# Fused linear attention and gated MLP on one core: fills, splits, load issues and transposes moved between engines and queues

## Chip, cores and metric

One core of one Trainium2 chip. The metric is the device time of one launch in microseconds (us). Kernels are timed in alternation with the kernel before on the same chip. The executions of one kernel over 1.5% above the fastest of the same kernel are classed as slow and left out of the ratios.

## The reference, cut to what matters

For 8 batches, 8 heads, 576 tokens and head width 64, the first stage is linear attention with features exp(p) and exp(-p), where p is a projection shifted by its largest absolute value. The second is an MLP whose gate mixes tokens.

```python
def phi(x):                                   # x: (8, 8, 576, 64), w_phi: (64, 128)
    proj = np.einsum('bhsd,df->bhsf', x, w_phi)
    proj = proj - np.max(np.abs(proj), axis=-1, keepdims=True)
    return np.concatenate([np.exp(proj), np.exp(-proj)], axis=-1)
q_p, k_p = phi(q), phi(k)
kv = np.einsum('bhsf,bhsd->bhfd', k_p, v)     # and num / den with z = sum of k_p
...
h = np.maximum(x @ w_in, 0.0)                 # x: attention output, (8, 576, 512)
u, v = h[..., :512], h[..., 512:]             # v: layer norm, then a 576 x 576 token mix plus bias
gated = u * v_s
return gated @ w_out
```

## The kernel before

The work is cut into 36 units: 32 pairs of heads over the first 512 tokens of a batch, and 4 tail units that hold the last 64 tokens of two batches. Unit i is worked on in step i (keys and queries) and in the next three or four (features, sums, attention, transpose of the attention output). Tasks of the second stage wait in a list and fill TensorE between the parts of a step. After the last step the rest of the list is drained.

Four places matter. The loads of a tail or a batch, with their transposes by DMA behind them in the sync engine's queue (SP):

```python
def load_heads(b, h0, n):
    for x, t in (("k", k), ("q", q)):
        pin(nc.gpsimd.dma_start)(out=src, in_=main_ap(t, b, h0, n))       # casts to bf16
        if b >= XB:                                                       # XB = 2
            pin(nc.sync.dma_start_transpose)(out=d[x + "T"][...], in_=src...)
# load_tail(g): the same for tails: k, q by GpSimd, transposes and v by sync
# load(b): alloc, load_heads(b, 0, H), v by GpSimd for b < 2, else by sync
```

The fills of constants and, before the first unit's work is through, ten copies of bias rows, all on VectorE or left to the compiler:

```python
nc.vector.memset(vst_i, 0.0)                     # twice, 128 x 2112 bf16
nc.any.memset(vnt_i, 0.0); nc.any.memset(vnt_i[TL:TL + 1, 0, :], 1.0); ...
nc.vector.tensor_copy(out=w_spT[row, NB + bl, ...], in_=bsp_row[...])   # ten of these
```

The split of the query maxima into two bf16 parts, and the transpose of the attention output:

```python
def a_split(u):
    eng = nc.vector if u["i"] < EARLY else nc.gpsimd             # EARLY = 4
    eng.tensor_copy(out=m[:, 0:H], in_=u["mq"])                  # mq is fp32 in SBUF
    eng.tensor_tensor(out=m[:, H:2 * H], in0=u["mq"], in1=m[:, 0:H], op=ALU.subtract)

def a_x_t(u):
    if XX <= u["i"] < NU - 4:                                    # XX = 9
        nc.sync.dma_start_transpose(out=dst..., in_=u["x"]...)
        return
    # else four TensorE transposes into PSUM and one VectorE copy
```

## Time and profile before

| | |
|---|---|
| time, median of three | 302.22 us (300.67 to 305.91) |
| profiled span | 300.1 us |
| busiest engines | TensorE 87%, ScalarE 75%, VectorE 71% |
| step 0 starts (first key maximum) | 10.7 us |
| step 7 starts | 48.1 us |
| last step, 35, starts | 236.7 us |

The starts of the steps I take from VectorE's timeline: every unit begins with two reductions that give the maxima of its keys. The page and the views of this profile that carry the argument are shown in the prediction.

### The profile page before, as it was taken

The numbers are of one execution on the slowest core, as the hardware profiler recorded it, in microseconds if no ns is written. First come the engines' busy times: TensorE is split into PE (matmuls) and PEld (weight loads), VectorE is DVE, ScalarE is ACT, GpSimd is POOL, SyncE is SP. The second block draws the span as 40 slices with busy tenths as digits, with TensorE's granted clock in tenths as the row PEclk, the third lists the DMA queues.
The fourth block names the chain that finished last, engine by engine and source line by source line (L and its number), as shares of the span: only waits on it lengthen the run. The fifth ranks groups of instructions, "written<-read, shape, count | busy, mean of one in ns | idle before, by whom it ended". The sixth has DMA issues, their size and how long they took to land.

```text
span 300.1 us, 7883 instructions
## 1 busy us (share of the span) xinstructions
PE 262.3 (87%) x3007; PEld 180.4 (60%) x3046; DVE 211.9 (71%) x512; ACT 224.1 (75%) x512; POOL 184.1 (61%) x324
## 2 busy tenths in 40 slices
PE   2356888999999999779999995979999999999983
PEld 1235777576766766556667673656767667545441
DVE  5999889797968877549697883656788864445610
ACT  4336899878699997769999675879999837566033
POOL 9398388589635998447879962814988430048300
PEclk9999999999999999999999997999999999999998
DMA  9999999909952899999612999999303202600026
GB/s 142 245 153 268 166 111 159 262 1 123 215 190 75 109 166 233 152 280 162 136 21 28 185 211 224 142 305 235 81 1 37 20 2 69 226 26 0 0 84 233
DMA packets 82906, 41.10 MB, mean 137 GB/s; under 512 B 53490, under 2 KB 77234, under 8 KB 82868
## 3 DMA queue, kind: packets, MB, share of 16 engines
q1 hardware_dynamic: 55524, 27.08, 41.9%
q0 software_dynamic: 27344, 13.51, 33.1%
q8 instruction: 24, 0.39, 0.6%
q14 instruction: 14, 0.11, 0.1%
HBM read 32.85 MB, written 9.44 MB: 141 GB/s over the span
## 4 chain that ended last, share of the span: by engine, by line
PE 56%; DVE 16%; ACT 14%; DMA 8%; issue 3%; SPq 1%; ACTq 0%; DVEq 0%
PE ps L476 9%; PE pv L402 7%; PE pu L455 6%; PE po L499 6%; PE ps L236 6%; DMA out_dram<-ob 5%; ACT kf L251 5%; PE pn L353 3%; DVE mk L248 3%; DVE mq L257 3%; PE pv L333 3%; ACT qf L320 3%; PE pq L303 3%; PE pq L307 3%; PE ps L477 2%
## 5 line engine op out<-in xcount | busy, mean ns | idle before, releaser
L251 ACT ACTIVATE kf<-ps 128x512 bf16<-128x512 f32 x144 | 76.8, 667 | 19.4 <-DVE mk L248 19.1
L320 ACT ACTIVATE qf<-pq 128x512 bf16<-128x512 f32 x128 | 68.0, 667 | 13.6 <-PE pq L307 13.6
L268 POOL TENSOR_TENSOR vs<-v_f,em 128x512 bf16<-128x512 f32 x64 | 65.6, 1047 | 15.7 <-ACT em L263 15.5
L248 DVE TENSOR_REDUCE mk<-ps 128x4 f32<-128x512 f32 x72 | 46.1, 678 | 9.5 <-PE ps L236 9.2
L257 DVE TENSOR_REDUCE mq<-ps 128x4 f32<-128x512 f32 x72 | 46.3, 679 | 3.1 <-PE ps L236 2.7
L501 ACT COPY ob<-po 128x512 f32<-128x512 f32 (+1 forms) x37 | 21.6, 597 | 25.7 <-PE po L499 17.2
L405 DVE BATCH_NORM_STATS2 stats<-vr 128x6 f32<-128x512 bf16 (+1 forms) x37 | 25.2, 685 | 17.6 <-ACT vr L404 17.5
L402 PE MATMUL pv<-w_in_bf,xT 128*128 128x512 bf16 x119 | 31.2, 379 | 2.2 <-DMA xT<-x 1.7
L476 PE MATMUL ps<-w_spT,vn 128*128 128x512 bf16 x117 | 32.3, 379 | 0.6
L455 PE MATMUL pu<-xT,w_in_bf 128*128 128x512 bf16 x120 | 30.8, 379 | 0.7 <-DVE mq L257 0.3
L307 PE MATMUL pq<-mT,sel 128*128 128x128 bf16 x256 | 30.7, 222 | 0.0
L499 PE MATMUL po<-w_out_bf,uT 128*128 128x512 bf16 x121 | 29.7, 379 | 0.4 <-issue 0.2
L479 DVE TENSOR_TENSOR uT<-ps,uT 128x512 bf16<-128x512 f32 x32 | 22.1, 691 | 11.0 <-PE ps L477 9.7
L307 PEld LDWEIGHTS <-sel 128*128 128x128 bf16 x256 | 25.4, 99 | 6.5 <-issue 2.2
L344 DVE TENSOR_TENSOR x<-pn,rc 128x256 bf16<-128x256 f32 x64 | 25.8, 419 | 1.0
L287 POOL CAST mhl<-mq 128x8 bf16<-128x8 f32 x32 | 6.2, 192 | 33.1 <-DVE mq L257 29.3
L404 ACT ACTIVATE vr<-pv 128x512 bf16<-128x512 f32 (+1 forms) x37 | 23.2, 680 | 4.2 <-PE pv L402 3.3
L333 PE MATMUL pv<-vs,kf 128*128 128x66 bf16 x512 | 25.0, 195 | 0.0
L419 POOL TENSOR_SCALAR vn<-vr,rs 128x512 bf16<-128x512 bf16 x32 | 24.3, 772 | 0.8
L333 PEld LDWEIGHTS <-kf 128*128 128x128 bf16 x512 | 23.9, 99 | 1.0
L353 PE MATMUL pn<-kv,qf 128*128 128x66 bf16 x512 | 22.2, 193 | 2.0 <-ACT kf L251 0.9
L353 PEld LDWEIGHTS <-qf 128*128 128x128 bf16 x512 | 19.4, 97 | 6.0 <-issue 2.5
(127 smaller groups left out, 547.5 us busy)
## 6 DMA issues: line engine op xcount, KB each, us to landing
out_dram<-ob SPq DMA_DIRECT2D x32, 256.0 KB, 2.7
v_f<-in_v_dram SPq DMA_DIRECT2D x6, 1024.0 KB, 6.8
k_bf<-in_k_dram POOLq DMA_DIRECT2D x7, 512.0 KB, 6.7
q_bf<-in_q_dram POOLq DMA_DIRECT2D x7, 512.0 KB, 8.3
v_f<-in_v_dram POOLq DMA_DIRECT2D x2, 1024.0 KB, 8.5
v_tl<-in_v_dram SPq DMA_DIRECT2D x8, 128.0 KB, 4.2
w_in_bf<-in_moe_w_in_dram POOLq DMA_DIRECT2D x1, 1024.0 KB, 12.5
out_dram<-ob SPq DMA_DIRECT2D x8, 128.0 KB, 2.9
```

The source lines that it names most:

```text
L248: nc.vector.tensor_reduce(out=u["mk"][:, hs], in_=pk, axis=AX.X, op=ALU.max, apply_absolute_value=True)
L251: nc.scalar.activation(out=u["kf"][:, s, hs, :], in_=pk, func=AF.Exp, bias=0.0, scale=sc)
L257: nc.vector.tensor_reduce(out=u["mq"][:, 4 * half:4 * half + 4], in_=pq, axis=AX.X, op=ALU.max, apply_absolute_value=True)
L268: nc.gpsimd.tensor_tensor(out=vs[:, s, :, 0:D], in0=st[u["b"]]["v"][:, pj * H:(pj + 1) * H, :], in1=em[:, s, :].unsqueeze(2).to_broadcast( ...
L307: nc.tensor.matmul(out=pq[:, 2 * par + x, :], lhsT=sel[:, j, :], rhs=m, start=False, stop=(x == 1))
L320: nc.scalar.activation(out=qf[:, s], in_=pq, func=AF.Exp, bias=0.0, scale=sc)
L333: nc.tensor.matmul(out=pv[:, hh, s, :], lhsT=u["kf"][:, s, 4 * hh + c, :], rhs=u["vs"][:, s, 4 * hh + c, :], start=(c == 0), stop=False)
L353: nc.tensor.matmul(out=pn[:, pos, :], lhsT=u["qf"][hh][:, s, pos, :], rhs=d["kv"][:, 2 * u["pj"] + hh, s, :], start=(s == 0), stop=(s == 1))
L402: nc.tensor.matmul(out=pv[r], lhsT=lhs(kc), rhs=w_in_bf[:, kc, HALF:DFF], start=(kc == 0), stop=(kc == KC - 1))
L455: nc.tensor.matmul(out=pu, lhsT=w_in_bf[:, kc, dc * P:(dc + 1) * P], rhs=d["xT"][:, kc, :], start=(kc == 0), stop=(kc == KC - 1))
L476: nc.tensor.matmul(out=ps, lhsT=d["vn"][:, sp, cs], rhs=w_spT[:, sp, 0:T0], start=(sp == 0), stop=False)
L499: nc.tensor.matmul(out=po[r], lhsT=lhs(dc), rhs=w_out_bf[:, dc, :], start=(dc == 0), stop=(dc == KC - 1))
```

## The change

Its intent: to shorten the start, which VectorE bounds, and to take waiting transposes out of the sync queue, where stores stand behind them. The diff, cut to its core (left out: the projection's weights load from ScalarE's queue, the constants are filled in a fixed order, and half of the first tail's multiplies move to step 4):

```diff
-    TS, TB = 1, 1                      # load_tail, load: issued whole, transposes behind them
+    def load(x, b, h0=0, n=H): ...     # one operand at a time
+    def cross(b):                      # transposes of a whole batch, released on their own
+        for x in ("k", "q"): pin(nc.sync.dma_start_transpose)(out=d[x + "T"], in_=d[x]...)
...
+        pin(nc.scalar.copy)(out=vst_i, in_=zero.to_broadcast([P, 4 * H * DA]))
+        pin(nc.scalar.copy)(out=vnt_i[:, bl, :], in_=ident[:, row:row + 1].to_broadcast([P, HALF]))
...
+    load_v(0, nc.sync)                 # was: GpSimd's queue, behind tails and heads 2 and 3
+    for x in ("k", "q", "v"):
+        load_tail(x, 0)
+    load("k", 0, 2, 2); load("q", 0, 2, 2); load("k", 0, 4, 4); load("q", 0, 4, 4)
...
-    EARLY = 4; XX = 9
+    EARLY = 5; XX = 99; EK = 7         # EK: early key copies by VectorE
-            for pos, c in enumerate(POS): nc.vector.tensor_copy(... bias row ...)
+            pin(nc.scalar.copy)(... bias row, two instructions for each of two rows ...)
...
+            if early and half == 0:
+                mq = pq[:, 0, 0:H]     # the early maxima stay in PSUM and are split from there
...
-    RATE = 3.23; CAP = 1.76
+    RATE = 3.12; CAP = 2.11            # and another order of the parts of a step
...
+    AT, AB, XP = 4, 5, 2
+    at(1, load, "k", 1); at(1, load, "q", 1); at(1, load_v, 1, nc.sync)
+    at(2, load_weight, w_in_bf[:, :, HALF:DFF], ...) ; at(3, ...wsp...) ; at(4, ...)
+    # tails: k four steps ahead, q and v three; batches: k five ahead, q and v four,
+    # cross(b) two ahead; tails have no DMA transpose any more, TensorE does them
```

More of the change, by code (lines that the diff above doesn't have):

```diff
@@ L60, in pin @@
     def pin(start):
-        return lambda **kw: tc.keep_in_program_order(start(**kw))
+        return lambda *a, **kw: tc.keep_in_program_order(start(*a, **kw))
     def main_ap(t, b, h0=0, n=H):
@@ L72 @@
     gs = {}
-    TS, TB = 1, 1
     XB = 2
-    def load_tail(g):
-        d = dict(
-            q=ld.tile([P, H, D], BF16, tag="q_tl", name="q_tl", bufs=1),
-            k=ld.tile([P, H, D], BF16, tag="k_tl", name="k_tl", bufs=1),
-            v=ld.tile([P, H, D], FP32, tag="v_tl", name="v_tl", bufs=1),
-        )
-        gs[g] = d
-        for x, t in (("k", k), ("q", q)):
-            for i in range(2):
-                pin(nc.gpsimd.dma_start)(out=d[x][i * TL:(i + 1) * TL], in_=tail_ap(t, 2 * g + i))
-            if 2 * g >= XB:
-                d[x + "T"] = ld.tile([P, NP, P], BF16, tag=x + "T_t", name=x + "T_t", bufs=1)
-                pin(nc.sync.dma_start_transpose)(out=d[x + "T"], in_=d[x].rearrange("p h d -> p (h d)"))
-        for i in range(2):
-            pin(nc.sync.dma_start)(out=d["v"][i * TL:(i + 1) * TL], in_=tail_ap(v, 2 * g + i))
     def alloc(b):
@@ L98, in alloc, with alloc_tail @@
         )
-        if b >= XB:
-            for x in ("kT", "qT"):
-                st[b][x] = ld.tile([P, 2 * H, P], BF16, tag=x + "_b", name=x + "_b", bufs=2)
-    def load_heads(b, h0, n):
-        d = st[b]
-        for x, t in (("k", k), ("q", q)):
-            src = d[x][:, h0:h0 + n]
-            pin(nc.gpsimd.dma_start)(out=src, in_=main_ap(t, b, h0, n))
-            if b >= XB:
-                pin(nc.sync.dma_start_transpose)(out=d[x + "T"][:, 2 * h0:2 * (h0 + n), :],
-                                            in_=src.rearrange("p h x -> p (h x)"))
+    def alloc_tail(g):
+        gs[g] = dict(
+            q=ld.tile([P, H, D], BF16, tag="q_tl", name="q_tl", bufs=1),
+            k=ld.tile([P, H, D], BF16, tag="k_tl", name="k_tl", bufs=1),
+            v=ld.tile([P, H, D], FP32, tag="v_tl", name="v_tl", bufs=1),
+        )
@@ L112, in load_v, with load, load_tail @@
+    def load(x, b, h0=0, n=H):
+        if b not in st:
+            alloc(b)
+        pin(nc.gpsimd.dma_start)(out=st[b][x][:, h0:h0 + n], in_=main_ap(q if x == "q" else k, b, h0, n))
     def load_v(b, eng):
         pin(eng.dma_start)(out=st[b]["v"].rearrange("p (h c) d -> p h (c d)", h=H), in_=main_ap(v, b))
-    def load(b):
-        alloc(b)
-        load_heads(b, 0, H)
-        load_v(b, nc.gpsimd if b < 2 else nc.sync)
+    def load_tail(x, g):
+        if g not in gs:
+            alloc_tail(g)
+        t, eng = dict(q=(q, nc.gpsimd), k=(k, nc.gpsimd), v=(v, nc.sync))[x]
+        for i in range(2):
+            pin(eng.dma_start)(out=gs[g][x][i * TL:(i + 1) * TL], in_=tail_ap(t, 2 * g + i))
@@ new lines, in cross @@
+    def cross(b):
+        d = st[b]
+        for x in ("k", "q"):
+            d[x + "T"] = ld.tile([P, 2 * H, P], BF16, tag=x + "T_b", name=x + "T_b", bufs=2)
+            pin(nc.sync.dma_start_transpose)(out=d[x + "T"], in_=d[x].rearrange("p h x -> p (h x)"))
+    wphi_f = cpool.tile([P, F], FP32)
+    for i in range(2):
+        nc.scalar.dma_start(out=wphi_f[i * D:(i + 1) * D, :], in_=w_phi)
+    alloc(0)
+    first = {}
+    for x, t in (("k", k), ("q", q)):
+        first[x] = s2.tile([P, 2, NB * D], FP32, tag="ob", name="first", bufs=4)
+        pin(nc.sync.dma_start)(out=first[x], in_=main_ap(t, 0, 0, 2))
@@ L121 @@
     ident = cpool.tile([P, P], BF16)
     make_identity(nc, ident)
-    alloc(0)
-    for x, t in (("k", k), ("q", q)):
-        first = s2.tile([P, 2, NB * D], FP32, tag="ob", name="first", bufs=4)
-        nc.sync.dma_start(out=first, in_=main_ap(t, 0, 0, 2))
-        nc.vector.tensor_copy(out=st[0][x][:, 0:2], in_=first)
-    wphi2 = cpool.tile([P, 2 * F], BF16)
-    nc.vector.memset(wphi2, 0.0)
-    wphi_f = cpool.tile([P, F], FP32)
-    for i in range(2):
-        r = slice(i * D, (i + 1) * D)
-        nc.sync.dma_start(out=wphi_f[r, :], in_=w_phi)
-        nc.vector.tensor_copy(out=wphi2[r, i * F:(i + 1) * F], in_=wphi_f[r, :])
@@ L135 @@
-    load_tail(0)
-    load_heads(0, 2, 2)
-    load_v(0, nc.gpsimd)
-    load_heads(0, 4, 4)
+    zero = cpool.tile([P, 1], BF16)
+    pin(nc.vector.memset)(zero, 0.0)
+    wphi2 = cpool.tile([P, 2 * F], BF16)
+    pin(nc.vector.memset)(wphi2, 0.0)
+    neghalf = cpool.tile([P, NB + 1], FP32)
+    pin(nc.vector.memset)(neghalf, -0.5)
+    w_spT = cpool.tile([P, NB + 2, S], BF16)
+    pin(nc.vector.memset)(w_spT[:, NB:NB + 2, :], 0.0)
+    NM = 3
+    mhl, mT = [], []
+    for i in range(NM):
+        for tiles, name in ((mhl, "mhl"), (mT, "mT")):
+            t = cpool.tile([P, P], BF16, name=f"{name}{i}")
+            pin(nc.vector.memset)(t, 0.0)
+            tiles.append(t)
@@ new lines @@
+    sel1 = cpool.tile([P, H], BF16)
+    sel = cpool.tile([P, H, F], BF16)
+    pin(nc.vector.tensor_tensor)(out=sel1, in0=ident[:, 0:H], in1=ident[:, H:2 * H], op=ALU.add)
+    pin(nc.vector.tensor_scalar)(out=sel, in0=sel1.unsqueeze(2).to_broadcast([P, H, F]), scalar1=-1.0,
+                                 scalar2=None, op0=ALU.mult)
+    for x in ("k", "q"):
+        pin(nc.vector.tensor_copy)(out=st[0][x][:, 0:2], in_=first[x])
+    vst, vnt = [], []
+    for i in range(2):
+        t = cpool.tile([P, 2, 2, H, DA], BF16, name=f"vst{i}")
+        pin(nc.scalar.copy)(out=t.rearrange("p b s h d -> p (b s h d)"), in_=zero.to_broadcast([P, 4 * H * DA]))
+        vst.append(t)
+        if i == 0:
+            for y in range(2):
+                r = slice(y * D, (y + 1) * D)
+                pin(nc.scalar.copy)(out=wphi2[r, y * F:(y + 1) * F], in_=wphi_f[r, :])
+        t = cpool.tile([P, 2, HALF], BF16, name=f"vnt{i}")
+        for bl, row in ((0, TL), (1, 0)):
+            pin(nc.scalar.copy)(out=t[:, bl, :], in_=ident[:, row:row + 1].to_broadcast([P, HALF]))
+        vnt.append(t)
@@ L140 @@
+    load_v(0, nc.sync)
+    for x in ("k", "q", "v"):
+        load_tail(x, 0)
+    load("k", 0, 2, 2)
+    load("q", 0, 2, 2)
+    load("k", 0, 4, 4)
+    load("q", 0, 4, 4)
     w_in_bf = cpool.tile([P, KC, DFF], BF16)
     w_out_bf = cpool.tile([P, KC, DM], BF16)
-    w_spT = cpool.tile([P, NB + 2, S], BF16)
     wsp = s2.tile([P, NB, T0], BF16, tag="vn", name="wsp", bufs=2)
@@ L148, with load_weight @@
     nc.sync.dma_start(out=bsp_row[0:1, :], in_=moe_b_spatial)
-    def load_weights():
-        pin(nc.gpsimd.dma_start)(out=w_in_bf, in_=moe_w_in.rearrange("(kc p) f -> p kc f", p=P))
-        rows = moe_w_spatial[0:T0, :].rearrange("(p c) s -> p c s", c=NB)
-        pin(nc.gpsimd.dma_start)(out=wsp, in_=rows[:, :, 0:T0])
-        pin(nc.gpsimd.dma_start)(out=wspr, in_=rows[:, :, T0:S])
-        pin(nc.gpsimd.dma_start)(out=wspt, in_=moe_w_spatial[T0:S, :])
-        pin(nc.gpsimd.dma_start)(out=w_out_bf, in_=moe_w_out.rearrange("(kc p) f -> p kc f", p=P))
-    sel1 = cpool.tile([P, H], BF16)
-    sel = cpool.tile([P, H, F], BF16)
-    nc.vector.tensor_tensor(out=sel1, in0=ident[:, 0:H], in1=ident[:, H:2 * H], op=ALU.add)
-    nc.vector.tensor_scalar(out=sel, in0=sel1.unsqueeze(2).to_broadcast([P, H, F]), scalar1=-1.0,
-                            scalar2=None, op0=ALU.mult)
-    neghalf = cpool.tile([P, NB + 1], FP32)
-    nc.vector.memset(neghalf, -0.5)
-    NM = 3
-    EARLY = 4
-    XX = 9
-    mhl, mT = [], []
-    for i in range(NM):
-        t = cpool.tile([P, P], BF16, name=f"mhl{i}")
-        nc.vector.memset(t, 0.0)
-        mhl.append(t)
-        t = cpool.tile([P, P], BF16, name=f"mT{i}")
-        nc.vector.memset(t, 0.0)
-        mT.append(t)
-    vst, vnt = [], []
-    for i in range(2):
-        t = cpool.tile([P, 2, 2, H, DA], BF16, name=f"vst{i}")
-        nc.vector.memset(t, 0.0)
-        vst.append(t)
-        t = cpool.tile([P, 2, HALF], BF16, name=f"vnt{i}")
-        nc.any.memset(t, 0.0)
-        nc.any.memset(t[TL:TL + 1, 0, :], 1.0)
-        nc.any.memset(t[0:1, 1, :], 1.0)
-        vnt.append(t)
-    nc.any.memset(w_spT[:, NB:NB + 2, :], 0.0)
+    rows = moe_w_spatial[0:T0, :].rearrange("(p c) s -> p c s", c=NB)
+    cols = moe_w_in.rearrange("(kc p) f -> p kc f", p=P)
+    def load_weight(out, in_):
+        pin(nc.gpsimd.dma_start)(out=out, in_=in_)
+    EARLY = 5
+    XX = 99
+    EK = 7
     def transpose_spatial(i):
@@ L209, in transpose_spatial @@
         for bl, row in ((0, TL), (1, 0)):
-            for pos, c in enumerate(POS):
-                nc.vector.tensor_copy(out=w_spT[row:row + 1, NB + bl, pos * P:(pos + 1) * P],
-                                      in_=bsp_row[row:row + 1, bass.ds(c, P, step=NB)])
-            nc.vector.tensor_copy(out=w_spT[row:row + 1, NB + bl, T0:S], in_=bsp_row[row:row + 1, T0:S])
+            r = slice(row, row + 1)
+            pin(nc.scalar.copy)(
+                out=w_spT[r, NB + bl, 0:T0].rearrange("o (a b p) -> o a b p", a=2, b=2),
+                in_=bsp_row[r, 0:T0].rearrange("o (p b a) -> o a b p", a=2, b=2))
+            pin(nc.scalar.copy)(out=w_spT[r, NB + bl, T0:S], in_=bsp_row[r, T0:S])
     def a_transpose(u):
@@ L221, in a_transpose @@
             return
-        for x, copy in (("k", nc.scalar.copy), ("q", nc.vector.tensor_copy)):
+        for x, copy in (("k", nc.vector.tensor_copy if u["i"] < EK else nc.scalar.copy), ("q", nc.vector.tensor_copy)):
             pt = psum.tile([P, 4, P], BF16, tag="bank", name="pt")
@@ L253, in a_queries @@
     def a_queries(u):
-        u["mq"] = small.tile([P, H], FP32, tag="mq", name="mq")
+        m, early = mhl[u["i"] % NM], u["i"] < EARLY
+        if not early:
+            mq = small.tile([P, H], FP32, tag="mq", name="mq")
         for half in range(2):
             pq = by_token(u["qT"], half)
-            nc.vector.tensor_reduce(out=u["mq"][:, 4 * half:4 * half + 4], in_=pq, axis=AX.X, op=ALU.max,
+            if early and half == 0:
+                mq = pq[:, 0, 0:H]
+            nc.vector.tensor_reduce(out=mq[:, 4 * half:4 * half + 4], in_=pq, axis=AX.X, op=ALU.max,
                                     apply_absolute_value=True)
+        eng = nc.vector if early else nc.gpsimd
+        eng.tensor_copy(out=m[:, 0:H], in_=mq)
+        eng.tensor_tensor(out=m[:, H:2 * H], in0=mq, in1=m[:, 0:H], op=ALU.subtract)
     def a_scale(u):
-        em = small.tile([P, 2, H], FP32, tag="em", name="em")
+        em = small.tile([P, 2, H], FP32, tag="em" if u["pair"] else "em_t", name="em", bufs=3 if u["pair"] else 1)
         for s, sc in ((0, -1.0), (1, 1.0)):
@@ L273, in a_scale, with tail_scale @@
             d = gs[u["g"]]
-            vs = vst[u["g"] % 2]
-            for bl in range(2):
-                r = slice(bl * TL, (bl + 1) * TL)
-                for s in range(2):
-                    nc.gpsimd.tensor_tensor(out=vs[r, bl, s, :, 0:D], in0=d["v"][r],
-                                            in1=em[r, s, :].unsqueeze(2).to_broadcast([TL, H, D]), op=ALU.mult)
-                nc.gpsimd.tensor_copy(out=vs[r, bl, :, :, D:D + 1].rearrange("p i n o -> p i (n o)"), in_=em[r])
-            d["vs"] = vs
-            d["unit"] = u
-    def a_split(u):
-        m = mhl[u["i"] % NM]
-        eng = nc.vector if u["i"] < EARLY else nc.gpsimd
-        eng.tensor_copy(out=m[:, 0:H], in_=u["mq"])
-        eng.tensor_tensor(out=m[:, H:2 * H], in0=u["mq"], in1=m[:, 0:H], op=ALU.subtract)
+            d["vs"], d["unit"], d["em"] = vst[u["g"] % 2], u, em
+            for bl in range(2 if u["i"] > 1 else 1):
+                tail_scale(u["g"], bl)
+    def tail_scale(g, bl):
+        d = gs[g]
+        vs, em = d["vs"], d["em"]
+        r = slice(bl * TL, (bl + 1) * TL)
+        for s in range(2):
+            nc.gpsimd.tensor_tensor(out=vs[r, bl, s, :, 0:D], in0=d["v"][r],
+                                    in1=em[r, s, :].unsqueeze(2).to_broadcast([TL, H, D]), op=ALU.mult)
+        nc.gpsimd.tensor_copy(out=vs[r, bl, :, :, D:D + 1].rearrange("p i n o -> p i (n o)"), in_=em[r])
     def a_max_t(u):
@@ L557, in b_tasks @@
         return ts
-    ORDER = (("keys", 0.375), ("queries", 0), ("sums", 0), ("next", 0.125),
-             ("attention", 0.5), ("features", 0), ("maxima", 0), ("out", 0))
-    RATE = 3.23
-    CAP = 1.76
+    ORDER = (("keys", 0.375), ("queries", 0.25), ("attention", 0), ("sums", 0.25),
+             ("next", 0.125), ("features", 0), ("out", 0), ("maxima", 0))
+    RATE = 3.12
+    CAP = 2.11
     LAGS = dict(next=-1, maxima=1, features=2, sums=2, attention=3, out=4)
@@ L572, in fill @@
             credit[0] -= cost
+    FT = dict(next=-1, maxima=1, features=2)
     def lag(u, what):
-        return (FIRST if u["pair"] and u["b"] == 0 or u["i"] == 1 else LAGS).get(what, 0)
+        return (FT if u["i"] == 1 else FIRST if u["pair"] and u["b"] == 0 else LAGS).get(what, 0)
     def step(i):
@@ L592, in step @@
                     a_queries(u)
-                    a_split(u)
                 elif what == "next":
@@ L616, in finish_batch, with at @@
             f(g, [0, 1])
+    AT, AB, XP = 4, 5, 2
+    io = {}
+    def at(i, f, *a):
+        io.setdefault(i, []).append(lambda: f(*a))
+    at(1, load, "k", 1)
+    at(1, load, "q", 1)
+    at(1, load_v, 1, nc.sync)
+    at(2, load_weight, w_in_bf[:, :, HALF:DFF], cols[:, :, HALF:DFF])
+    at(3, load_weight, wsp, rows[:, :, 0:T0])
+    at(3, load_weight, wspr, rows[:, :, T0:S])
+    at(3, load_weight, wspt, moe_w_spatial[T0:S, :])
+    at(4, tail_scale, 0, 1)
+    at(4, load_weight, w_in_bf[:, :, 0:HALF], cols[:, :, 0:HALF])
+    at(4, load_weight, w_out_bf, moe_w_out.rearrange("(kc p) f -> p kc f", p=P))
+    for u in units:
+        if not u["pair"] and u["g"] > 0:
+            at(u["i"] - AT, load_tail, "k", u["g"])
+            at(u["i"] - AT + 1, load_tail, "q", u["g"])
+            at(u["i"] - AT + 1, load_tail, "v", u["g"])
+        if u["pair"] and u["pj"] == 0 and u["b"] > 1:
+            at(u["i"] - AB, load, "k", u["b"])
+            at(u["i"] - AB + 1, load, "q", u["b"])
+            at(u["i"] - AB + 1, load_v, u["b"], nc.sync)
+            if u["b"] >= XB:
+                at(u["i"] - XP, cross, u["b"])
     for i in range(NU + 4):
-        u = unit(i)
         step(i)
-        if i == 0:
-            load(1)
-            load_weights()
-        if u and u["pair"] and u["pj"] == NP - 1 and u["b"] + 2 < B:
-            load(u["b"] + 2)
-        if u and u["pair"] and u["pj"] == TS and u["b"] % 2 == TB and u["g"] + 1 < G:
-            load_tail(u["g"] + 1)
+        for f in io.get(i, []):
+            f()
     while queue:
```

## The prediction

> **What bounds the kernel now.** I read the page first, then the chain of waits, then the busy time by stretch, then VectorE's order of work in the first 32 us, and last the waits of the sync queue.
>
> The page: TensorE is the busiest engine, but its busy time is stretched by pipelining, so I count its columns instead.
>
> ```profile
> span 300.1 us, 7883 instructions
> ...
> PE 262.3 (87%) x3007; PEld 180.4 (60%) x3046; DVE 211.9 (71%) x512; ACT 224.1 (75%) x512; POOL 184.1 (61%) x324
> ```
>
> The chain gives the rate of a matmul that waits for nothing, and the three places in mid-run where the chain leaves the engines (columns: start us, length us, what):
>
> ```profile
> 121.42 1.62 SPq L362
> 123.14 6.56 DMA out_dram<-ob
> ...
> 176.84 6.19 DMA kT_t<-k_tl
> ...
> 195.22 3.13 DMA out_dram<-ob
> ...
> 272.44 3.45 PE pu L455 x16
> ```
>
> Sixteen 512-column matmuls in 3.45 us is 0.42 ns a column; the 66-column ones run 16 in 0.50 us, 31 ns each. The recorded matmuls at these rates are 237 us; some 35 of the 512-column matmuls that the program has are missing from the trace (119, 117, 120 and 121 of 128 each in four groups), another 8 us. So TensorE has about 245 us of work in 300 and some 55 us of true idleness. Where it lies:
>
> ```profile
> core 0: us, PE busy (x) PEld busy (x) DVE busy (x) ACT busy (x) POOL busy (x), PEclk, DMA share, GB/s
> 0.00:10.00 10.00, 2.22 (x12) 1.19 (x12) 6.48 (x20) 3.07 (x4) 8.35 (x16) 1.00 1.05 161
> 10.00:20.00 10.00, 4.74 (x29) 3.41 (x29) 9.74 (x22) 4.92 (x14) 6.20 (x8) 1.00 1.13 193
> 20.00:30.00 10.00, 6.99 (x45) 5.32 (x46) 9.73 (x18) 5.38 (x14) 9.16 (x13) 1.00 1.17 252
> ...
> 120.00:140.00 20.00, 16.39 (x186) 11.25 (x186) 11.68 (x30) 15.76 (x36) 10.66 (x19) 1.00 1.28 202
> ...
> 180.00:200.00 20.00, 15.66 (x155) 10.33 (x159) 9.92 (x22) 13.06 (x31) 9.26 (x15) 0.91 1.26 221
> ```
>
> From 10 to 30 us VectorE is 97% busy and TensorE half idle: the start is bound by VectorE. From 40 us TensorE sets the pace, except in 120 to 140 and 180 to 200, where every engine sags and the DMA engines are full. Counted in columns, TensorE does 13.4 us of work in the first 40 us, 15.5 in 120 to 140 and 13.7 in 180 to 200, against 18 to 19 in the other middle stretches. After 256 us only the second stage's matmuls are left and TensorE is full until the drain.
>
> What VectorE does at the start (start, length, operation):
>
> ```profile
> 6.17 0.94 DVE L182 MEMSET vst<- 128x1056 uint32 x1 [0.28 <-issue]
> ...
> 15.06 1.03 DVE L213 CAST w_spT<-bsp_row 1x64 bf16<-1x64 f32 x1
> 16.12 1.05 DVE L211 CAST w_spT<-bsp_row 1x128 bf16<-1x128 f32 x1
> ...
> 19.83 1.27 DVE L287 CAST mhl<-mq 128x8 bf16<-128x8 f32 x1
> ...
> 21.14 0.97 DVE L288 TENSOR_TENSOR mhl<-mq,mhl 128x8 bf16<-128x8 f32 x1
> ...
> 31.39 0.16 DVE L287 CAST mhl<-mq 128x8 bf16<-128x8 f32 x1
> ```
>
> The reader should compare the two casts of L287: 1.27 us against 0.16 us for the same eight columns. The slow ones lie where GpSimd multiplies or issues loads. The sync queue's own waits:
>
> ```profile
> SPq L61 <- DMA k_bf<-in_k_dram: 75.8, 6, 39.5
> SPq L513 <- ACT ob L501: 48.4, 3, 27.3
> SPq L362 <- DVE mv L406: 21.6, 2, 12.7
> ```
>
> The queue that stores the output also stands waiting for a key load before it may transpose it. Stores and attention transposes behind it wait too.
>
> **What the Trainium skill says.** "SBUF — State Buffer", section "SBUF: two separate sides": VectorE and GpSimd share a port pair by an exclusive lock; a VectorE instruction in a two-port mode, such as an fp32 copy from SBUF to SBUF, waits for a whole GpSimd instruction. The trace agrees: 0.16 us becomes 1.27 us, where a GpSimd multiply takes 1.05. "VectorE: DVE Perf Modes", section "Why PSUM operands drop a tier": PSUM offers one read port, so an operand there keeps the instruction out of the two-port modes. This trace has no split from PSUM; the copy of maxima out of PSUM (L293) averages 0.23 us, which fits. "DMA: Bandwidth & Descriptors", section "Rules for kernel authors": issuing from more engines brings no bandwidth, it only saves issue time. So I give moving v to the sync queue nothing but GpSimd's 0.93 us per issue. "TensorE: Matmul & The Clock Gate", section "Part 4: PE-mode transpose" puts a transpose at about 275 ns in context; this trace shows 220 ns each when recorded alone and 0.22 us for four in a row in the chain, and I use the latter.
>
> **The change part by part.**
> Start. Off VectorE go two fills at 0.94 us (1.9), four one-row fills at 0.48 (1.9), ten bias casts (3.7 + 2.1 = 5.8). The four early splits cost 4.1 us (1.8 + 2.3); at 0.16 us an instruction from PSUM they cost 1.3, saving 2.8. That is 12.4 us, nearly all before 32 us. On VectorE come seven early key copies of 0.42 us, 2.9, and a fill of w_spT, some 0.6 by its size. ScalarE takes the fills: 512 columns took it 0.63 us and 576 took 0.67, so 2,112 columns cost about 2 us by that slope, two of them 4 us, plus four row fills at 0.6. It is idle until 11.4 us now, so nearly all hides. Net: 8 to 9 us off the VectorE line that sets the start. As a check, VectorE's list for a first step is two key maxima and two query maxima (2.4), split 0.3, two copies 0.8, and from the second on mT 0.2 and kv 0.4: 3.6 to 4.2 us, with attention 5.0 to 5.7. Seven steps make 32 us. The first key maximum comes at 10.7 us now and at about 7 after; step 7 starts at 48.1 now and at about 39 after. I book 8.5 us.
>
> Middle. A step (one pair of heads) takes about 6.4 us undisturbed, from the starts of the key maxima. Four steps around the stalls take 9.3, 8.5, 10.1 and 9.5, together 11.8 us too much. Without 20 attention transposes and six tail transposes the sync queue has only stores, v, and twelve key and query transposes of about 3.1 us issue each. I book 9 of the 11.8, since a pair of those transposes still holds up stores for some 6 us, with four output buffers.
>
> Added to TensorE: 80 transposes of attention output and 24 of tails, 104 at 0.054 us = 5.6 us. TensorE sets the pace there, so all of it counts. VectorE gets 20 copies at 0.42 (8.4) and 3 of tails (1.2). Its middle steps go from about 5.4 us to 5.8, still under 6.4, so these are hidden. ScalarE's key copies fall from nine to five. The fill rate goes from 3.23 to 3.12. Adding up the tasks that the program releases before step 35 gives 86.0 us of second-stage work before and 84.9 after, so 1.1 us more remains for the end.
>
> Sum: 300.1 - 8.5 - 9 + 5.6 + 1.1 = 289.3 us of span. The new order of the parts of a step, and splits that no longer hold up GpSimd's issues, should give back some of the other 20 us of middle idleness; I book 4. That is 285, and the timed figure lies 1.8 above the profiled span (301.85 against 300.1): about 287.
>
> **The rivals.** (a) The start becomes bound by loads. For: the DMA engines are full through the first 30 us, and k, q, v and weights for two batches must come in. Against: the burst now carries weights whose first use is after step 7; ordered by need, batch 1 must be there by some 24 us. If it holds, only 3 us of the start is won: about 292. (b) The key transposes, now issued only two steps ahead, arrive late. They take about 7 us to land, the second about 3 later, and a step is 6.4. Where stores block the queue this costs 1 to 2 us for each of six batches: about 294. For it speaks the store wait of 6.56 us; against it, that without stores the queue runs ahead to the landing of the load. (c) ScalarE or VectorE becomes the bound in the middle. ScalarE does 20.00 us of 20 in 200 to 220 now; but that is catching up after a stall, for in 60 to 120 it has 16 to 18. If it were so, the added copies would cost 4 us more: 291. (d) The stalls vanish altogether and the start follows VectorE's list exactly: 280.
>
> **Range and chances.** The gain has two independent parts of 8 to 10 us, each of which could fail by half, against a sure cost of 5.6. One half failing gives 291 or 292, both failing 296. Predicted 287, range 279 to 296. Faster by over 2% (below 296.2) 0.86, within 2% 0.12, slower 0.02.
>
> **What would show it.** The first key maximum at about 7 us and the eighth unit's near 39; splits of 0.2 us on VectorE; no bias cast on it. No piece of the chain on the output stores between 100 and 200 us over 3 us, and no such sag in busy time there. TensorE with 104 more transposes and about 250 us of columns; after the last key maximum the same 63 us as now. Wrong it would be if the start is not shorter with VectorE freed (then loads bind it), if keys wait for their DMA transposes several times by over 1 us, or if the step without a stall grows beyond 6.7 us.

## The result, and the profile after

The changed kernel takes 292.63 us (median of four, 292.07 to 295.47) against 301.84 for the kernel before in the same rounds. The ratio is 0.9717 with a 95% interval of 0.964 to 0.9793: faster by 2.8%. Ratios here are the mean time of one kernel's fast runs over that of the other's of the same rounds, so they are not quite the ratios of the medians. The profiled execution happened to be the slowest of the four, 295.47 us; the spans of two others are 289.7 and 289.8.

The page of the changed kernel, to be held against the two lines shown of before:

```profile
span 293.0 us, 8088 instructions
...
PE 266.6 (91%) x3150; PEld 183.9 (63%) x3150; DVE 206.2 (70%) x529; ACT 229.9 (78%) x517; POOL 182.2 (62%) x320
```

The chain of waits of the changed kernel, its three longest pieces outside the engines before the drain (start, length, what):

```profile
3.79 12.25 DMA q_tl<-in_q_dram
...
120.69 6.91 DMA qT_b<-q_bf
...
182.35 6.74 DMA out_dram<-ob
```

The first was not there before: for 12 us the chain waits for the queries of the first tail. The other two are of the kind that the change was to remove. The busy time by stretch (the columns are those of the prediction's view; a DMA share near or above 1 means full DMA engines) shows the hole that the first piece makes:

```profile
10.00:20.00 10.00, 4.08 (x29) 3.01 (x29) 4.23 (x10) 4.64 (x13) 2.21 (x3) 1.00 1.21 199
20.00:30.00 10.00, 7.70 (x96) 6.48 (x94) 8.21 (x26) 7.20 (x21) 9.73 (x13) 0.83 0.79 103
...
120.00:140.00 20.00, 18.57 (x249) 13.16 (x247) 14.82 (x42) 18.13 (x43) 14.99 (x24) 1.00 1.00 194
...
180.00:200.00 20.00, 19.38 (x244) 13.54 (x243) 13.52 (x37) 18.29 (x44) 11.89 (x20) 1.00 0.90 202
```

VectorE was 97% busy from 10 to 20 us and is now 42% busy there, with the DMA engines full. From 20 to 30 us TensorE's granted clock is 0.83, where it was 1.00 before; what that costs was not measured. The sags at 120 and 180 us are mostly filled. VectorE's timeline (start, length, operation, and in brackets the idle time before it with what ended it) shows the first unit's key maxima and, nearly 10 us later, the copy of the tail's transposed queries, before which VectorE had been idle, and a split of 0.16 us from PSUM:

```profile
7.07 1.29 DVE L244 TENSOR_REDUCE mk<-ps 128x4 f32<-128x512 f32 x2 [0.80 <-PE ps L232]
...
16.80 0.42 DVE L227 COPY qT<-pt 128x512 bf16<-128x512 bf16 x1 [2.25 <-PE pt L225]
17.14 0.16 DVE L261 CAST mhl<-ps 128x8 bf16<-128x8 f32 x1
```

Why the tail is late stands in the sync queue's timeline (start, length of the issue, what it loads):

```profile
1.73 0.47 SPq L61 DMA_DIRECT2D v_f<-in_v_dram  x1
2.24 1.89 SPq L61 DMA_DIRECT2D v_tl<-in_v_dram  x2
...
5.14 1.98 SPq L61 DMA_DIRECT2D v_f<-in_v_dram  x1
```

Two loads of v, 1 MB each, leave the sync queue at 1.73 and at 5.14 us; the tail's queries were issued on GpSimd in between, from 3.12 us on. The second is batch 1's, which the program writes behind step 1. This kernel gives the sync engine nothing to compute, so nothing holds it back until that step is reached. The load is spread over steps in the text only. On GpSimd, which multiplies in every step, the spreading works: batch 1's keys were issued at 22.3 us.

From the starts of the steps (us), with 24 of the 28 steps from 7 to 35 set apart from the four in which the kernel before stalled (17, 18, 26 and 29):

| profile | step 0 | step 1 | step 7 | step 35 | the four steps, sum | each of the 24 others | span |
|---|---|---|---|---|---|---|---|
| before | 10.7 | 17.1 | 48.1 | 236.7 | 37.3 | 6.30 | 300.1 |
| changed | 7.1 | 17.2 | 44.1 | 228.6 | 28.6 | 6.50 | 293.0 |

So the gain of 7.1 us of span is 4.0 in the start and 8.7 in the four stalls, less 4.7 in the other steps, and less 1.0 after step 35 (64.4 us in place of 63.4).

### The profile page after: what moved, and what is told of

Its sections match the earlier page's. It is cut to its first block, busy times and chain, and to the rows that moved or that the text cites.

```text
span 293.0 us, 8088 instructions
## 1 busy us (share of the span) xinstructions
PE 266.6 (91%) x3150; PEld 183.9 (63%) x3150; DVE 206.2 (70%) x529; ACT 229.9 (78%) x517; POOL 182.2 (62%) x320
## 4 chain that ended last, share of the span: by engine, by line
PE 62%; ACT 12%; DVE 11%; DMA 11%; POOL 2%; issue 2%; SPq 0%; ACTq 0%; POOLq 0%; DVEq 0%
PE pv L403 11%; PE ps L477 8%; PE pu L456 7%; PE po L500 6%; PE ps L232 6%; DMA q_tl<-in_q_dram 4%; ACT qf L321 4%; DMA out_dram<-ob 4%; PE pv L334 4%; ACT kf L247 4%; PE pn L354 3%; PE pq L308 3%; PE pq L304 3%; DVE mk L244 3%; DMA qT_b<-q_bf 2%; PE ps L478 2%
## 5 line engine op out<-in xcount | busy, mean ns | idle before, releaser
L272 POOL TENSOR_TENSOR vs<-v_f,em 128x512 bf16<-128x512 f32 x64 | 65.6, 1049 | 22.9 <-ACT em L267 22.3
L321 ACT ACTIVATE qf<-pq 128x512 bf16<-128x512 f32 x128 | 67.3, 647 | 9.9 <-PE pq L308 9.9
L258 DVE TENSOR_REDUCE mq<-ps 128x4 f32<-128x512 f32 x62 | 39.9, 677 | 5.0 <-PE ps L232 4.4
L406 DVE BATCH_NORM_STATS2 stats<-vr 128x6 f32<-128x512 bf16 (+1 forms) x37 | 24.8, 687 | 14.5 <-ACT vr L405 14.4
L456 PE MATMUL pu<-xT,w_in_bf 128*128 128x512 bf16 x128 | 31.5, 379 | 0.0
L500 PE MATMUL po<-w_out_bf,uT 128*128 128x512 bf16 x128 | 30.4, 379 | 0.0
L480 DVE TENSOR_TENSOR uT<-ps,uT 128x512 bf16<-128x512 f32 x32 | 21.8, 683 | 11.9 <-PE ps L478 11.9
L369 DVE COPY xT<-pt 128x512 bf16<-128x512 bf16 x32 | 13.4, 419 | 20.3 <-PE pt L368 20.3
L405 ACT ACTIVATE vr<-pv 128x512 bf16<-128x512 f32 (+1 forms) x37 | 22.2, 638 | 5.0 <-PE pv L403 4.8
L354 PEld LDWEIGHTS <-qf 128*128 128x128 bf16 x512 | 20.3, 97 | 7.8 <-issue 1.4
L345 DVE TENSOR_TENSOR x<-pn,rc 128x256 bf16<-128x256 f32 x64 | 24.6, 416 | 0.3
L334 PEld LDWEIGHTS <-kf 128*128 128x128 bf16 x512 | 21.9, 98 | 1.9 <-issue 1.3
```

The costliest lines, as they stand in the source:

```text
L258: nc.vector.tensor_reduce(out=mq[:, 4 * half:4 * half + 4], in_=pq, axis=AX.X, op=ALU.max, apply_absolute_value=True)
L272: nc.gpsimd.tensor_tensor(out=vs[:, s, :, 0:D], in0=st[u["b"]]["v"][:, pj * H:(pj + 1) * H, :], in1=em[:, s, :].unsqueeze(2).to_broadcast( ...
L321: nc.scalar.activation(out=qf[:, s], in_=pq, func=AF.Exp, bias=0.0, scale=sc)
L334: nc.tensor.matmul(out=pv[:, hh, s, :], lhsT=u["kf"][:, s, 4 * hh + c, :], rhs=u["vs"][:, s, 4 * hh + c, :], start=(c == 0), stop=False)
L354: nc.tensor.matmul(out=pn[:, pos, :], lhsT=u["qf"][hh][:, s, pos, :], rhs=d["kv"][:, 2 * u["pj"] + hh, s, :], start=(s == 0), stop=(s == 1))
L456: nc.tensor.matmul(out=pu, lhsT=w_in_bf[:, kc, dc * P:(dc + 1) * P], rhs=d["xT"][:, kc, :], start=(kc == 0), stop=(kc == KC - 1))
```

## The experiments

The runs were made partly on different chips; the medians of the kernel before lie between 300.7 and 301.8 us. v_late, xx9, double and xp3 share their runs of before (median 301.19), so do v1_pool, v01_pool, b_xx99 and b_fills (300.93), and v01_xx9, v01_taildma and v01_split (300.68); combo ran by itself (301.30). With many rounds, before also had fast single runs (296.2), so more of its runs count as slow and its fast mean is lower. Ratios are therefore compared with care, and medians are quoted first.

### v_late: batch 0's v behind the small loads

```diff
-    load_v(0, nc.sync)
     for x in ("k", "q", "v"): load_tail(x, 0)
     load("k", 0, 2, 2); load("q", 0, 2, 2)
+    load_v(0, nc.gpsimd)
```

> Changed kernel, but batch 0's 1 MB of v goes back to GpSimd's queue, behind the tails and heads 2 and 3. Theory (v ahead of the small tail loads fills the DMA engines, so the tail queries land at 16 us and the second unit starts at 17.2): its first key maximum comes at about 11, step 7 moves from 44.1 to about 40, and the end from 292.6 to 288 or 289. Rival (the start is bound by the bytes of all loads together, in whatever order): the second unit comes earlier but a later step waits instead, step 7 stays within 1 us of 44 and the end within 1 us of 292.6.

Measured: 291.69 us, ratio 0.9687 (0.9611 to 0.9764). Step 1 starts at 12.8 us in place of 17.2, but step 3 only at 24.4 and step 7 at 42.1. GpSimd's timeline shows the new wait:

```profile
16.20 2.04 POOL L272 TENSOR_TENSOR vs<-v_f,em 128x512 bf16<-128x512 f32 x2 [4.02 <-DMA v_f<-in_v_dram]
```

The tails are early, but now batch 0's v, issued at 5.86 us, lands at 16 us: batch 1's v had gone out from the sync queue at 4.02 us. That this is the reason is shown by v01_pool below. Step 7 misses both ranges. The end lies about where the rival put it. The edit alone is worth nothing that these runs could separate.

### v1_pool: batch 1's v behind its own keys and queries

```diff
-    at(1, load_v, 1, nc.sync)
+    at(1, load_v, 1, nc.gpsimd)
```

> Changed kernel, but the v of batch 1 (not of batch 0) goes back to GpSimd's queue, behind that batch's k and q. Theory (the sync queue does not wait for the steps, so this 1 MB went out at 5.1 us, and two v loads together delay what the first steps need): batch 1's v is issued after 20 us, the tail queries land about 3 us earlier than 16, step 1 starts at about 14, step 7 at 41 or earlier, end 289 to 291. Rival (batch 0's v alone fills the engines until the tails have landed): step 1 stays within 1 us of 17.2, end within 1 us of 292.6.

Measured: 291.72 us, ratio 0.9789 (0.9719 to 0.9859). Step 1 starts at 16.4 and step 7 at 42.0. The rival was right: batch 0's v alone, ahead of the tails, keeps them out. The chain still has this piece:

```profile
3.79 11.39 DMA q_tl<-in_q_dram
```

### v01_pool: both

> Changed kernel with both v loads of batches 0 and 1 on GpSimd's queue, in order of need. Theory (what is left of the start's delay with only batch 0 moved, 4 us of GpSimd waiting for v at 12 to 16 us, is batch 1's v in the engines): first v lands at about 13, step 3 starts at about 21 in place of 24.4, step 7 at 38 to 39 as predicted from VectorE's list, end 287 to 289. Rival (bytes bind: the wait moves to heads 4 to 7 or to batch 1's keys): step 7 at 41 to 42, end 290 to 292.

Measured: 287.83 us (287.56 to 288.60), ratio 0.9665 (0.9596 to 0.9735). All four runs lie below all four of the changed kernel. The expectation held. Step 1 starts at 10.4, step 3 at 21.0 and step 7 at 38.7, where VectorE's list had put it at 39. VectorE's timeline of this kernel has the second unit's first key maximum here:

```profile
10.43 0.68 DVE L244 TENSOR_REDUCE mk<-ps 128x4 f32<-128x512 f32 x1
```

In GpSimd's timeline the first multiply by v waits 1 us for its load, where it waited 4.02 in v_late:

```profile
13.15 2.04 POOL L272 TENSOR_TENSOR vs<-v_f,em 128x512 bf16<-128x512 f32 x2 [0.97 <-DMA v_f<-in_v_dram]
```

Neither repair alone moved step 7 clear of the spread (42.1 and 42.0, where four profiles without a repair have 41.5 to 44.1); both together moved it to 38.7, and to 39.4 and 39.2 in v01_xx9 and v01_taildma below, which have the same start. The two waits ended at about the same time, so removing one uncovered the other. The same bytes in another order are enough: the start was bound by order, not by the sum of bytes.

### xx9: attention output by DMA again

```diff
-    XX = 99
+    XX = 9
```

> Changed kernel, but from unit 9 on the attention output is transposed by DMA again, as before the change (20 of them). Theory (the transposes in the sync queue cause the stalls at 120 and 180 us, TensorE's 4.3 us is the price of removing them): the long store or transpose waits of 5 us and more come back, end 296 to 299. Rival (the gain of the middle comes from the later issue of key transposes and the new order of a step, and the TensorE transposes cost what they save): 291 to 293.

Measured: 293.11 us (289.32 to 298.13, the last a slow run), ratio 0.9697 (0.9609 to 0.9785), no different from the changed kernel. The time speaks for the rival. But the chain has two long waits, as the theory had said:

```profile
142.97 5.82 DMA qT_b<-q_bf
...
185.29 8.58 DMA out_dram<-ob
```

Steps 23 and 29 take 10.0 and 9.9 us, against 6.1 and 7.4 in the changed kernel. So with these transposes two stalls came back in this profile, and TensorE pays about as much for removing them. The start of this profile, with the same code, was also 2.6 us earlier.

### b_xx99: the kernel before with this one part

```diff
-    XX = 9
+    XX = 99
```

> Kernel before with one part alone: all attention outputs transposed by TensorE. Theory (these transposes in the sync queue made the stalls; the work costs about 4 us on TensorE): the long waits on stores at 121 and on the tail transpose at 176 us go or shrink to under 3 us, end 294 to 299. Rival (the pairs of key transposes issued early, which wait for their load in the queue, hold up the stores just as well): the stalls stay, end 301 to 305.

Measured: 304.53 us, ratio 1.0208 (1.0124 to 1.0293): slower than before, by 3.6 us (1.2%) in the medians. Its chain still leaves the engines where before's did, and for as long:

```profile
123.16 8.96 DMA out_dram<-ob
179.53 6.55 DMA kT_t<-k_tl
```

The four stalled steps take 35.7 us (37.3 before), the others 6.48 each (6.30 before). So the attention transposes in the sync queue were not needed for these stalls, and moving them to TensorE costs 0.18 us a step. Over 24 steps that is 4.3 us, which is what 80 transposes at 0.054 us come to. This is one profile of each kernel.

### double: every attention transpose twice

```diff
-        for pos in range(NB):
-            nc.tensor.transpose(out=pt[:, pos, :], in_=u["x"][:, pos]..., identity=ident)
+        for pos in range(2 * NB):
+            nc.tensor.transpose(out=pt[:, pos % NB, :], in_=u["x"][:, pos % NB]..., identity=ident)
```

> Changed kernel with every attention output transposed twice on TensorE into the same place, same result: 128 more transposes, 6.9 us at 0.054 each. Theory (TensorE's columns set the pace of the middle, so the change's 104 transposes cost their full 5.6 us): end 5.5 to 7 us later, about 299. Rival (they lie in gaps that ScalarE and VectorE leave): under 3 us later, 293 to 295.

Measured: 297.94 us (297.39 to 298.35), ratio 0.9898 (0.9846 to 0.9950), 5.3 us over the changed kernel's median. The 128 extra transposes are 6.9 us of columns, so 77% of added TensorE time shows up in the end (5.3 over 6.9). It falls just short of the range that I had given for the theory, and far from the rival.

### v01_xx9: attention output by DMA, with the start repaired

The edits of v01_pool and xx9 together.

> Changed kernel with both early v loads on GpSimd's queue (287.8) and the attention output of units 9 to 31 transposed by DMA again. Theory as corrected (TensorE's transposes cost some 4 us of pace, and the stalls come from key, query and tail transposes in the sync queue, not from these): without new stalls 284 to 286; with the two stalls that the like kernel without the v repair showed, 287 to 290. Rival (my first one, that these transposes make the stalls and TensorE's are worth it): 291 or more.

Measured: 286.74 us (284.63 to 288.10), ratio 0.9566 (0.9506 to 0.9625). That falls between the two ranges of the theory and refutes the rival. It lies 1.1 us under v01_pool with ranges that overlap. Up to step 28 its profile is 2.9 us ahead of v01_pool's (174.22 against 177.16), then it loses that again behind stores:

```profile
174.94 6.99 DMA out_dram<-ob
...
182.65 6.05 DMA out_dram<-ob
```

So TensorE's attention transposes avoid a stall of about the size of their own price. On the whole they are worth nothing here.

### v01_taildma: tails by DMA, with the start repaired

```diff
+    def cross_tail(g):
+        for x in ("k", "q"):
+            pin(nc.sync.dma_start_transpose)(out=d[x + "T"], in_=d[x]...)
+            at(u["i"] - XP, cross_tail, u["g"])          # XP = 2
```

> Changed kernel with both early v loads on GpSimd's queue (287.8) and the tails of batches 2 to 7 transposed by DMA, two steps ahead, in place of TensorE. Theory (the waits of 6 us on a tail transpose at 176 us before and the queue's extra load are what this part removes): a wait on the tail's transpose of over 1 us in the chain, end 288.5 to 291. Rival (two steps ahead is early enough, and TensorE saves 24 transposes, 1.3 us): 286 to 288.

Measured: 295.18 us, ratio 0.9833 (0.9766 to 0.9900): 7.4 us worse than v01_pool, more than I had expected. Its chain:

```profile
38.68 9.46 DMA k_tl<-in_k_dram
48.20 8.30 DMA kT_t<-k_tl
121.71 8.11 DMA qT_b<-q_bf
185.72 6.62 DMA out_dram<-ob
```

The tail's transpose waits in the queue for its load, and TensorE then waits for the tail: steps 8 and 9 take 10.4 and 9.7 us, against 7.6 and 7.3 in v01_pool. This is not exactly the arrangement before, where the transposes were released right with the loads, but it is the same queue and the same order of load and transpose. So 24 small transposes on TensorE cost less than the waits that they replace here. But these waits lie in steps 8, 9 and 19 (11.0 us, against 6.0 in v01_pool). Steps 17, 18, 26 and 29, which stalled before, take 27.5 us, no more than the 28.4 of v01_pool. This run therefore does not show that the tails made the stalls of the kernel before. They took part in them: the chain of the kernel before waits on a tail's transpose at 176.84 us, and that of b_xx99 at 179.53.

### v01_split: early maxima split from SBUF

```diff
-        if not early:
+        if True:
             mq = small.tile([P, H], FP32, tag="mq", name="mq")
-            if early and half == 0: mq = pq[:, 0, 0:H]
```

> Changed kernel with both early v loads on GpSimd's queue (287.8) and the early maxima kept in SBUF, split from there by VectorE as before. Theory (GpSimd's multiplies hold up VectorE's fp32 casts from SBUF): some of the ten splits take 0.5 to 1.2 us in place of 0.16, in sum 2 to 4 us, step 7 1 to 3 us later than 38.7. Rival (with the fills gone the splits fall where GpSimd is idle): step 7 within 0.7 us, end within 1 us.

Measured: 288.65 us (287.98 to 289.53), ratio 0.9635 (0.9583 to 0.9687): 0.8 us over v01_pool, whose range overlaps. Step 7 starts at 40.5, 1.8 us later than v01_pool's and 1.1 later than v01_xx9's. Three of the ten splits are slow, these two among them:

```profile
19.80 1.12 DVE L259 CAST mhl<-mq 128x8 bf16<-128x8 f32 x1
20.96 1.07 DVE L260 TENSOR_TENSOR mhl<-mq,mhl 128x8 bf16<-128x8 f32 x1
```

GpSimd's timeline shows what the first of them lay beside. It ends at 20.93 us, with this issue of a load:

```profile
20.03 0.90 POOL L61 DMA_DIRECT2D v_f<-in_v_dram  x1
```

The second ends at 22.03, within 0.04 us of the end of a multiply. By these times VectorE waits not only for multiplies, as the theory had it, but also while GpSimd issues loads. The cost at the end is not clear of noise. Batch 0's v also landed 0.9 us later in this profile, so not all of the 1.8 us is the splits'.

### b_fills: the kernel before with fills and bias rows on ScalarE

```diff
-        nc.vector.memset(t, 0.0)                             # vst
+        pin(nc.scalar.copy)(out=t..., in_=zero.to_broadcast([P, 4 * H * DA]))
-        nc.any.memset(...)                                   # vnt, and rows of ones
+        pin(nc.scalar.copy)(out=t[:, bl, :], in_=ident[:, row:row + 1].to_broadcast([P, HALF]))
-        nc.vector.tensor_copy(out=w_spT[row, ...], ...)      # ten bias copies
+        pin(nc.scalar.copy)(...)                             # four
```

> Kernel before with one part alone: fills and bias rows by ScalarE as in the change. Theory (VectorE's list sets the start): step 7 starts at 41 to 43 in place of 48.1, end 295 to 298. Rival (the start waits for loads, or ScalarE's fills push the first exponentials back): step 7 not before 46, end 300 to 303.

Measured: 298.75 us (295.29 to 302.85 over 20 runs), ratio 0.9982 (0.9935 to 1.0029). In the profile step 7 starts at 42.5 us, 5.6 earlier, and 5.1 of it are still there at step 35. The profiled execution (296.62 us) was one of the faster, though. The medians differ by 2.2 us and the ratio by nothing. The start behaves as in the theory, and the end misses its range by 0.8 us; how much of the gain the end keeps stays open for this kernel, whose stalls vary from run to run.

### xp3: key and query transposes three steps ahead

```diff
-    AT, AB, XP = 4, 5, 2
+    AT, AB, XP = 4, 5, 3
```

> Changed kernel with the key and query DMA transposes released three steps ahead in place of two. Theory (a query transpose lands too late at 127 us and holds TensorE 1.4 to 1.9 us, twice in all, and the pairs of transposes meet the stores at 182): waits of TensorE on transposes go from about 4 us to under 1, end 289 to 292. Rival (the queue merely holds other stores then, the wait moves): within 1 us of 292.6.

Measured: 291.44 us (290.77 to 292.06), ratio 0.9683 (0.9629 to 0.9736). The wait on the query transpose at 120 us is gone from its profile. But it is gone from v_late's too, which releases them two steps ahead, so that wait comes and goes with the execution. A gain of about 1 us is possible and not shown.

### combo: five repairs at once

Both v loads as in v01_pool, XX = 9, XP = 3, five output buffers in place of four, and the bias rows at step 0.

> Five repairs to the changed kernel at once: both early v loads on GpSimd's queue, attention output of units 9 to 31 by DMA transposes, key and query transposes three steps ahead, five output buffers in place of four, and the bias rows written at step 0, where ScalarE is idle, not in step 9, where they took 2.5 us of it. Theory (the remaining stalls are stores behind transposes, 7.0 and 6.1 us of the chain in the like kernel with the first two alone): the chain's store waits between 100 and 200 us fall below 4 us, end 281 to 285. Rival (the queue is full of transposes there, one buffer and one step more move the wait only): 285 to 288.

Measured: 292.67 us (289.05 to 294.87), ratio 0.9656 (0.9573 to 0.9739); its profile fell in an execution classed as slow (292.5 us of span). Its median is 4.8 us above v01_pool's, the mean of its three fast runs 2.0 us above (290.0 against 288.0). Both my theory and the rival were wrong by either count. Its chain:

```profile
117.68 6.58 DMA xT<-x
...
187.66 8.78 DMA out_dram<-ob
```

The sync queue's timeline shows what the attention transpose of 117.68 stood behind:

```profile
107.48 5.88 SPq L61 DMA_TRANSPOSE kT_b<-k_bf  x1
114.56 3.02 SPq L61 DMA_TRANSPOSE qT_b<-q_bf  x1
117.68 1.22 SPq L365 DMA_TRANSPOSE xT<-x  x1
```

A key and a query transpose had the queue from 107.5 us on, and TensorE then waited 5.4 us for that attention transpose: a stall like those before, rebuilt. The fifth buffer did not prevent the wait on stores at 187.7. The bias rows at step 0 took ScalarE from 11.9 to 14.4 us, just when it was needed for the second unit's exponentials, and step 7 came at 40.4 in place of 38.7. As five edits changed at once, and the profile is of a slow execution, only what it shows at these places is told; why the fast runs are slower too stays open.

## Why the prediction was right or wrong

The prediction was 287 us with a range of 279 to 296. The measured 292.63 lies inside, 5.6 us above the centre, about where it had put the case that one of its two parts fails by half (291 or 292). The start did fail by half, and the give-back failed too. By its own steps:

**The start, booked at 8.5 us: too large, 4.0 in the profile.** The list of VectorE's work was right. The first key maximum came at 7.07 us (predicted about 7), the splits took 0.15 to 0.17 us, no bias cast was left on VectorE, and the big fills on ScalarE took 1.95 us each (about 2). Small slips did no harm: its slope of 0.04 us for 64 columns gives 1.6 us for such a fill, ScalarE was not idle until 11.4 us (busy 3.07 us of the first 10), the rise of EARLY to five adds a split and a copy to VectorE (some 0.7 us) that the sum leaves out, and the slow cast of 1.27 us lay beside GpSimd's issue of weight loads, not beside a multiply of 1.05. The step that failed is the sentence "So I give moving v to the sync queue nothing but GpSimd's 0.93 us per issue." Moving v changed when it goes out. One load of 1 MB (1.73 us) entered the DMA engines ahead of the tail's queries (3.12 us), the other (5.14 us) a step's work too early, and together they cost the start the difference. With both back behind what is needed first, step 7 starts at 38.7 us (predicted about 39). Rival (a), a start bound by loads, came nearest, but for another reason than bytes. The start also varies: three other profiles with the same start code (double, xp3, xx9) had step 7 at 43.1, 41.8 and 41.5.

**The stalls, booked at 9 us of 11.8: right in size, 8.7 (37.3 less 28.6), in part by luck, for the cause is not shown.** I had put the stalls down to 20 attention transposes and six tail transposes alike. Removing the 20 alone (b_xx99) took 1.6 us off the four steps and lost 3.6 us in all. Putting the 20 back (xx9) made two stalls in steps 23 and 29 and changed the time by nothing. Putting the tails alone back (v01_taildma) cost 7.4 us, in steps 8, 9 and 19; the four steps stayed at 27.5. So no single part shown here accounts for the 8.7 us. What is left is the later release of the key and query transposes, alone or together with the tails. xp3 moves it by one step and leaves the four steps at 28.8; the early release of the kernel before was not put back, so the cause stays open.

**TensorE's price, 5.6 us, "all of it counts": nearly right.** b_xx99 gives 0.18 us a step for the attention part, the full 4.3 us of 80 transposes; double gives 77% of the added columns. By these, 104 transposes cost 4.3 to 5.6 us.

**The 4 us of give-back: wrong.** "I book 4" for a better order of the parts of a step and for splits that do not hold up GpSimd was a guess with no row behind it. The 24 steps without a stall went from 6.30 to 6.50 us, 4.7 us in all, which is TensorE's price with no give-back or one of under 1 us. In v_late, v1_pool and xp3, with the same middle, they take 6.42 to 6.45, which would leave room for 1 to 3 us, not 4. No run changes the order of the parts alone.

**The end, 1.1 us more: right.** 64.4 us after the last key maximum in place of 63.4. TensorE's columns were put at about 250 us; the recorded ones of the changed kernel, at the prediction's rates, add up to some 250.

**Rivals (b) and (c).** A query transpose did come late once in the profiled run (120.69 us, 6.91 us of the chain) and once at another place in v1_pool's (87.56 us, 4.45 us), and not in v_late, v01_pool, double and xp3; it was no steady cost of 1 to 2 us for each batch. VectorE or ScalarE as the bound was not seen: adding TensorE work alone still moved the end by three quarters of it.

**The signs.** The first key maximum, the splits, the bias casts, the 104 more transposes (656 recorded matmuls of 128 columns in place of 552) and the 6.50 us of a step came as said. The eighth unit's start did not (44.1, not 39). Nor did "no piece of the chain on the output stores" over 3 us: the chain has 6.74 us at 182.35, and v1_pool's 7.06 at 180.53, though the steps there are not long.

The sum in the profile, 4.0 + 8.7 - 4.7 - 1.0 = 7.0, matches the 7.1 us of span. The profiled execution was 2.8 us slower than the median, which is why the span suggests less than the timed 9.2 us.

## What to carry to other kernels

In the sync queue, whose engine has nothing to compute here, a load written behind step 1 left at 5.14 us. So spread loads over steps only on a queue that the steps hold back, and keep big loads behind the small ones that are needed first. A transpose that waits for its load held everything behind it in its queue (75.8 us of waits on key loads before). Price each part of a change alone, and look where it acts: with the start repaired, keeping the tails' transposes out of the queue was worth 7.4 us and keeping the attention's out nothing, and neither alone explains the stalls of the kernel before. Repair two suspected waits together before calling either innocent: each alone was worth about 1 us at most, both 4.8.

## What the Trainium skill lacked or had wrong

- "DMA: Bandwidth & Descriptors", section "Rules for kernel authors", says that spreading transfers over issuing engines does not help bandwidth and saves only issue time. No run here tests the bandwidth. The section does not say that the choice of queue also sets when a load leaves: batch 1's v went out at 5.14 us from the sync queue and at 19.1 us from GpSimd's, and with batch 0's v moved too the end differs by about 5 us (292.63 against 287.83).
- The same page, section "Queues, rings and completion order", says that each DMA engine takes packets from its queues in turn. The section gives no figure for what a small load pays: the first tail's second query load (64 KB) took 12.25 us from issue to landing with 1 MB of v issued before it and 1 MB just behind it, and 4.56 us in v01_pool, where both v loads come later.
- "TensorE: Matmul & The Clock Gate", section "Part 4: PE-mode transpose", gives the latency of a single transpose (about 275 ns in context) and no cost in a stream. Four in a row took 0.22 us of the chain here, and 128 more of them cost 5.3 us of time, 41 ns each.
- "SBUF — State Buffer", section "SBUF: two separate sides", has a lock that fits these runs: the same eight-column cast took 1.12 us from SBUF beside GpSimd's issue of loads and 0.16 from PSUM, and its partner took 1.07 beside a multiply. The page tells of VectorE holding up GpSimd's issue of loads, not of the reverse that the 1.12 us shows. How little it may matter is not there either: all early splits together were worth about 0.8 us, not clear of noise.
